# One TensorE loop of eight rounds and new column shares for the DMA engines in a grouped 1x1 convolution

## The chip, the cores and the metric

The kernel runs on one core of one Trainium2 chip. The metric is the device time of one execution in microseconds (us). Most runs of one kernel agree within some 0.3%. Every experiment was timed in turns with the kernel before on the same chip. A ratio is always the mean time of one kernel's fast runs over that of the other's of the same rounds, so it is not quite the ratio of the medians quoted beside it.

## The reference

```python
H = W = 512; G = 4; Cg = 48; C = 192; k = 1
# x: (1, 512, 512, 192) bf16,  w: (1, 1, 4, 48, 48) bf16
xg = x.reshape(B, H, W, G, Cg)
out = einsum('bhwgc,gcd->bhwgd', xg, w[0, 0]).reshape(B, H, W, C)
```

Each of the 262,144 pixels has four groups of 48 channels, and each group is multiplied by its own 48x48 matrix. 100.7 MB are read and as many written, with little arithmetic for each byte.

## The kernel before

Pixels are spread over 128 SBUF rows (partitions). A "column" is one pixel on every row, 384 bytes in each. Loads go into a ring of three slots of 80 columns. Four columns are a "group" of the program: 6 transposes and 6 matmuls on TensorE, and one copy by ScalarE into an output ring of 280 columns, from which stores leave. Two groups are a "pair", the unit of TensorE's program; VectorE makes one copy for each pair, between the transposes and the matmuls.

Three parts matter here. First, the column plan. Most pieces have all 128 rows. The PARTIAL pieces leave out rows 16 to 19 and 48 to 51, so that these eight rows get fewer pixels; a REST piece gives 12 columns more to rows 0 to 15 alone:

```python
FULL = (("sync", 0, 128, 128),)
PARTIAL = (                                   # queue, first row, rows, outer
    ("sync", 0, 16, 4), ("sync", 32, 16, 4),
    ("pool", 52, 44, 11), ("pool", 20, 12, 3), ("pool", 96, 32, 8),
)
REST = (("sync", 0, 16, 4),)
FRONT = ((6, ((36, FULL), (44, PARTIAL))), (12, ((12, REST), (24, FULL), (44, PARTIAL))))
```

Second, the TensorE program. In this program a loop is possible only where every slot is one regular load of 80 columns, because the loop's wait for a slot has to be the same in each round. The mixed slots (36 + 44, and 12 + 24 + 44) break this, so there are two loops, of 2 and of 4 rounds of 30 pairs; 138 of the 258 pairs' instructions are written out:

```python
                for pair in range(pair, first):
                    step(pair)
                with pe.Fori(0, rounds):
                    for pair in range(first, first + body):
                        step(pair)
```

Third, the waits. TensorE waits for each piece's own semaphores at the piece's first group:

```python
                    if g == p.g0:
                        keys = [ld_key[p.i, n] for n in range(len(p.blocks))]
                        for key in keys:
                            pe.wait_ge(ld_sem[key], 16)
                        todo += keys if p.regular else []
```

## Time and profile before

The kernel before takes 479.06 us (median of 3 runs, 478.95 to 479.91). The profiled span is 477.7 us.

| what | value | read from |
|---|---|---|
| packets' time, all DMA queues | 99% of 16 engines' span | page, part 3 |
| TensorE busy, ScalarE busy | 430.9 us, 390.1 us | page, part 1 |
| fetches of TensorE instructions | 26 of 16 KB | page, part 3, queue q8 |
| ScalarE waits for stores to leave the output ring | 21.7 us | view of waits |
| TensorE waits for loads | 7.3 us (matmuls); the weight loads' 4.0 us is the longest of these waits seen once more | view of waits |

The page of the kernel before. PE and ACT are TensorE and ScalarE, PEld is TensorE's loading of weights, DVE is VectorE and POOL is GpSimd; the rows of part 2 are 40 equal slices of the span in tenths; part 3 has for each queue its packets, MB and share of the 16 engines' time.

```profile
span 477.7 us, 13632 instructions
PE 430.9 (90%) x6202; PEld 389.3 (81%) x6202; DVE 247.8 (52%) x259; ACT 390.1 (82%) x517; POOL 12.5 (3%) x28
DMA  8999999999999999999999999999999999999997
q1 hardware_dynamic: 4340, 97.71, 48.0%
q10 hardware_dynamic: 4996, 97.69, 47.9%
q0 software_dynamic: 1216, 5.95, 3.0%
q8 instruction: 26, 0.43, 0.3%
```

The DMA row has no hole: loads (q1), stores (q10) and the transfers of the partial pieces (q0) fill the 16 engines from start to end. Queue q8, of the kind "instruction", is taken for the one that brings TensorE's instructions: its packets have 16,384 bytes each. One such transfer is called a fetch here.

The view of waits of the kernel before, in us in total, times, and longest:

```profile
PEld o_ps L339 <- ACT oring L415: 60.1, 149, 3.7
ACT oring L415 <- DMA out_dram<-oring: 21.7, 10, 3.5
PE xT_ps L319 <- DMA ring<-in_x_dram: 7.3, 4, 3.8
PEld xT_ps L319 <- DMA ring<-in_x_dram: 4.0, 1, 4.0
```

The two kinds of wait on DMA are what compute's slack is spent on.

### The profile page before, as it was taken

Reading aid. Unit: us, or ns where it says so; the run is one execution under the profiler, and the core shown is the slowest. Engines: PE = TensorE matmul, PEld = TensorE weight load, DVE = VectorE, ACT = ScalarE, POOL = GpSimd, SP = SyncE. Lnnn points to the kernel's source line nnn. Section 1 sums busy time; section 2 is a strip of 40 time slices with the busy share of each in tenths; the row PEclk is TensorE's granted clock in tenths of the full one; section 3 lists DMA queues with packets and bytes.
Section 4 is the critical chain, followed back from the end, with each engine's and each line's share of the span. In section 5 each row is a group of like instructions: output and inputs, shape, how many; then the busy total and the mean of one; then the engine's idle time right before and its main releaser. Section 6 shows DMA issues by size and latency. Waiting matters only on the chain.

```text
span 477.7 us, 13632 instructions
## 1 busy us (share of the span) xinstructions
PE 430.9 (90%) x6202; PEld 389.3 (81%) x6202; DVE 247.8 (52%) x259; ACT 390.1 (82%) x517; POOL 12.5 (3%) x28
## 2 busy tenths in 40 slices
PE   5999999999986999999897997899997969979994
PEld 4988889888876898888796896789886868878883
DVE  2555555555543555555553554455554534635551
ACT  2898899988984998998895886799987858868885
POOL 1000000200002000000000000002000020000000
PEclk9999999999998999999998999999999989989997
DMA  8999999999999999999999999999999999999997
GB/s 325 445 403 432 417 426 429 438 427 431 427 428 432 437 420 433 425 436 430 434 434 423 435 435 433 430 429 430 425 431 430 428 426 433 420 432 429 423 401 302
DMA packets 10588, 201.85 MB, mean 423 GB/s; under 512 B 2105, under 2 KB 2105, under 8 KB 2649
## 3 DMA queue, kind: packets, MB, share of 16 engines
q1 hardware_dynamic: 4340, 97.71, 48.0%
q10 hardware_dynamic: 4996, 97.69, 47.9%
q0 software_dynamic: 1216, 5.95, 3.0%
q8 instruction: 26, 0.43, 0.3%
q14 instruction: 10, 0.07, 0.0%
HBM read 100.68 MB, written 100.66 MB: 421 GB/s over the span
## 4 chain that ended last, share of the span: by engine, by line
PE 56%; DMA 30%; ACT 9%; another core or an unknown queue 2%; issue 1%; ACTq 1%; SPq 0%
PE o_ps L339 32%; PE xT_ps L319 23%; DMA out_dram<-oring 21%; DMA ring<-in_x_dram 9%; ACT oring L415 9%; ACTq L396 1%; SPq L288 0%; SPq L281 0%; ACTq L389 0%; ACTq L398 0%
## 5 line engine op out<-in xcount | busy, mean ns | idle before, releaser
L415 ACT CAST oring<-o_ps 128x768 bf16<-128x768 f32 x516 | 388.8, 801 | 81.6 <-PE o_ps L339 53.0
L378 DVE COPY xT_sb<-xT_ps 128x1536 bf16<-128x1536 bf16 x258 | 247.1, 958 | 218.7 <-PE xT_ps L319 218.7
L339 PE MATMUL o_ps<-wt,xT_sb 128*128 128x144 bf16 (+1 forms) x3096 | 289.7, 236 | 30.4 <-ACT oring L415 25.0
L339 PEld LDWEIGHTS o_ps<-wt,xT_sb 128*128 128x128 bf16 x3096 | 212.7, 99 | 69.0 <-ACT oring L415 60.1
L319 PE MATMUL xT_ps<-ident,ring 128*128 128x128 bf16 x3096 | 222.3, 222 | 7.3 <-DMA ring<-in_x_dram 7.3
L319 PEld LDWEIGHTS xT_ps<-ident,ring 128*128 128x128 bf16 x3096 | 190.0, 99 | 10.2 <-DMA ring<-in_x_dram 4.0
L260 POOL DMA_DIRECT2D fill<-in_x_dram x8 | 4.6, 574 | 376.2 <-PE xT_ps L319 258.6
L268 POOL DMA_DIRECT2D ring<-in_x_dram x6 | 3.3, 560 | 0.0
L275 POOL DMA_DIRECT2D out_dram<-oring x6 | 3.3, 556 | 0.0
L300 PE MATMUL o_ps<-w_sb,esel 48*128 48x48 bf16 x10 | 0.6, 209 | 2.6 <-DMA w_sb<-in_w_dram 2.6
L300 PEld LDWEIGHTS o_ps<-w_sb,esel 48*128 48x128 bf16 x10 | 0.4, 111 | 2.6 <-POOL esel L247 2.6
L371 DVE CAST wt<-o_ps 128x480 bf16<-128x480 f32 x1 | 0.7, 657 | 3.2 <-PE o_ps L300 3.2
L415 ACT ACT_TABLE_LOAD x1 | 1.3, 1283 | 0.8 <-PEq L435 0.8
L247 POOL TENSOR_SCALAR_AFFINE_SELECT esel<-esel 48x272 bf16<-48x272 bf16 x1 | 0.4, 402 | 0.0
L244 POOL MEMSET esel<- 48x272 bf16 x1 | 0.3, 317 | 0.3 <-POOLq L435 0.3
L251 POOL TENSOR_SCALAR_AFFINE_SELECT ident<-ident 128x128 bf16<-128x128 bf16 x1 | 0.3, 282 | 0.0
L245 POOL MEMSET ident<- 128x128 bf16 x1 | 0.2, 197 | 0.0
L435 POOL MEMSET const-float32-0.0<- 128x1 f32 x1 | 0.1, 98 | 0.3 <-issue 0.3
L435 POOL MEMSET const-bfloat16-1.0<- 128x1 bf16 x1 | 0.1, 101 | 0.0
L435 POOL MEMSET const-uint8-127<- 128x1 uint8 x1 | 0.1, 101 | 0.0
L435 POOL MEMSET const-float32-1.0<- 128x1 f32 x1 | 0.1, 98 | 0.0
## 6 DMA issues: line engine op xcount, KB each, us to landing
ring<-in_x_dram SPq DMA_DIRECT2D x22, 3840.0 KB, 28.8
out_dram<-oring ACTq DMA_DIRECT2D x12, 3456.0 KB, 39.9
out_dram<-oring ACTq DMA_DIRECT2D x11, 3264.0 KB, 44.7
out_dram<-oring ACTq DMA_DIRECT2D x2, 2880.0 KB, 48.3
out_dram<-oring ACTq DMA_DIRECT2D x2, 1728.0 KB, 31.3
ring<-in_x_dram SPq DMA_DIRECT2D x1, 3072.0 KB, 21.6
ring<-in_x_dram SPq DMA_DIRECT2D x2, 1152.0 KB, 17.0
ring<-in_x_dram SPq DMA_DIRECT2D x1, 2304.0 KB, 11.1
```

What stands on the lines that cost most here:

```text
L247: gp.affine_select(out=esel[:], in_=esel[:], pattern=[[-1, ECOLS]], compare_op=AluOpType.is_equal, fill=0.0, base=ESHIFT, channel_multipli ...
L260: gp.dma_start(dst, src).then_inc(fill_sem[k], 16)
L268: gp.dma_start(sbuf, dram).then_inc(ld_sem[ld_key[p.i, n]], 16)
L275: gp.dma_start(dram, sbuf).then_inc(st_sem[i][n], 16)
L300: last = pe.matmul(o_ps[:, NOB - 1, col:col + CG], lhsT=esel[:, s0:s0 + 128], rhs=w_sb[:, g, :], start=True, stop=True, skip_group_check=True)
L319: last = pe.transpose(xT_ps[:, g % NXP, j * 128:(j + 1) * 128], xg[:, j * 128:(j + 1) * 128], ident[:])
L339: last = pe.matmul(o_ps[:, v % NOB, c0_:c1_], lhsT=xs[:, j * 128:(j + 1) * 128], rhs=wt[:, WOFF[tc]:WOFF[tc] + (c1_ - c0_)], start=(tc == ...
L371: dve.tensor_copy(wt[:], o_ps[:, NOB - 1, 0:WCOLS]).then_inc(wc_sem, 1)
L378: dve.tensor_copy(xT_sb[pair % NXS][:, 0:n * 2 * UC].rearrange("p (g c) -> p g c", g=n), xT_ps[:, b0:b0 + n, 0:2 * UC]).then_inc(e_done[pa ...
L396: act.dma_start(dram, sbuf).then_inc(st_sem[i][n], 16)
L415: act.copy(out_columns(g).rearrange("p (u c) -> p u c", u=2), o_ps[:, v % NOB:v % NOB + 2, 0:UC]).then_inc(fa_done[g % (2 * NTOK)] if g < ...
L435: nc = _bacc.Bacc("TRN2", target_bir_lowering=False, num_devices=1)
```

## The change

The intent: make the mixed slots look regular to TensorE, so that one loop of 8 rounds covers nearly the whole program. GpSimd waits for all DMAs of a mixed slot and then counts the slot's ordinary semaphore up. The partial pieces get 48 columns instead of 44. They now come first in their slot. The second has 16 columns fewer on rows 0 to 15, which also makes the pixel count come out. The rule that cuts the stores changes too; with the new columns the late ones come out finer. The core of the diff:

```diff
 PARTIAL = (
-    ("sync", 0, 16, 4), ("sync", 32, 16, 4),
-    ("pool", 52, 44, 11), ("pool", 20, 12, 3), ("pool", 96, 32, 8),
+    ("sync", 0, 16, 4, 0), ("sync", 32, 16, 4, 0),
+    ("pool", 52, 44, 11, 0), ("pool", 20, 12, 3, 0), ("pool", 96, 32, 8, 0),
 )
-REST = (("sync", 0, 16, 4),)
-FRONT = ((6, ((36, FULL), (44, PARTIAL))), (12, ((12, REST), (24, FULL), (44, PARTIAL))))
+UNEVEN = (("sync", 0, 16, 4, 16), *PARTIAL[1:])
+FRONT = ((6, ((48, PARTIAL), (32, FULL))), (11, ((48, UNEVEN), (32, FULL))))
 ... (a Unit is a slot with all its pieces; loop_spans now goes by units)
+                for p in u.pieces:                      # GpSimd
+                    for n in range(len(p.blocks)):
+                        gp.wait_ge(ld_sem[ld_key[p.i, n]], 16)
+                gp.sem_inc(ld_sem[unit_keys[u][0]], 16)
 ...
-                    if g == p.g0:                       # TensorE
-                        keys = [ld_key[p.i, n] for n in range(len(p.blocks))]
-                        for key in keys:
+                    if g == u.g0:
+                        for key in unit_keys[u]:
                             pe.wait_ge(ld_sem[key], 16)
-                        todo += keys if p.regular else []
+                        todo += unit_keys[u] if u.regular else []
 ... (stores: OGRID ends at least 24 columns on; short full fields in one store)
```

There are now 514 groups in 257 pairs, of which 47 are written out.

More of the change, by code (lines that the diff above doesn't have):

```diff
@@ L37 @@
 NTOK = 6
-FULL = (("sync", 0, 128, 128),)
+FULL = (("sync", 0, 128, 128, 0),)
 PARTIAL = (
-    ("sync", 0, 16, 4), ("sync", 32, 16, 4),
-    ("pool", 52, 44, 11), ("pool", 20, 12, 3), ("pool", 96, 32, 8),
-)
-REST = (("sync", 0, 16, 4),)
-FRONT = ((6, ((36, FULL), (44, PARTIAL))), (12, ((12, REST), (24, FULL), (44, PARTIAL))))
+    ("sync", 0, 16, 4, 0), ("sync", 32, 16, 4, 0),
+    ("pool", 52, 44, 11, 0), ("pool", 20, 12, 3, 0), ("pool", 96, 32, 8, 0),
+)
+UNEVEN = (("sync", 0, 16, 4, 16), *PARTIAL[1:])
+FRONT = ((6, ((48, PARTIAL), (32, FULL))), (11, ((48, UNEVEN), (32, FULL))))
 FILL_ROWS = 5
@@ L58, in __init__ @@
         self.blocks = []
-        for (queue, r0, rows, outer) in blocks:
-            self.blocks.append((queue, r0, rows, outer, pix))
-            pix += rows * cols
+        for (queue, r0, rows, outer, less) in blocks:
+            self.blocks.append((queue, r0, rows, outer, pix, cols - less))
+            pix += rows * (cols - less)
         self.pix_end = pix
@@ L73, in __init__ @@
         self.full, self.blocks = field.full, field.blocks
-        self.regular = self.full and size == BIG and self.at % BIG == 0
         assert size % 4 == 0 and self.at + size <= RCOLS
@@ L90, in plan_fields @@
         head = 0
-    cols = npix - sum(n * sum(b[2] for b in blocks) for n, blocks in parts)
+    cols = npix - sum((n - b[4]) * b[2] for n, blocks in parts for b in blocks)
     if cols < 128 * BIG:
@@ L128, in plan_stores @@
             if f.full:
-                end = min([g for g in OGRID if g > at]) - at + c
+                end = min([g for g in OGRID if g > at + 24] or [OCOLS]) - at + c
+                if f.cols < BIG:
+                    end = min(OCOLS - at + c, f.cols)
                 if ends and c >= f.cols - LATE_COLS:
@@ L137, in plan_stores, with __init__, plan_units, loop_spans @@
     return stores
-def loop_spans(pieces):
+class Unit:
+    def __init__(self, pieces):
+        self.pieces, self.g0, self.g1 = pieces, pieces[0].g0, pieces[-1].g1
+        self.slot = pieces[0].at // BIG
+        self.regular = pieces[0].at % BIG == 0 and 4 * (self.g1 - self.g0) == BIG
+def plan_units(pieces):
+    units, rest = [], list(pieces)
+    while rest:
+        n = 1
+        if rest[0].g0 and rest[0].at % BIG == 0:
+            while n < len(rest) and rest[n].at % BIG:
+                n += 1
+        units.append(Unit(rest[:n]))
+        rest = rest[n:]
+    return units
+def loop_spans(units):
     body, out, run = RCOLS // 4, [], []
-    for p in pieces + [None]:
-        if p and p.regular:
-            run.append(p)
+    for u in units + [None]:
+        if u and u.regular:
+            run.append(u)
             continue
@@ L165, in bass_standalone__grouped__vision_kernel @@
     stores = plan_stores(fields)
-    piece_of = {g: p for p in pieces for g in range(p.g0, p.g1)}
+    units = plan_units(pieces)
+    unit_of = {g: u for u in units for g in range(u.g0, u.g1)}
     store_of = {g: s for s in stores for g in range(s.g0, s.g1)}
@@ L169, in bass_standalone__grouped__vision_kernel @@
     NP = (NG + 1) // 2
-    LOOPS = loop_spans(pieces)
+    LOOPS = loop_spans(units)
     assert all(RCOLS // 4 % n == 0 for n in (2 * NXS, 2 * NTOK, NXP))
@@ L181, in transfers @@
         f, c0, c1, at = part.field, part.c0, part.c1, part.at
-        for n, (queue, r0, rows, outer, pix) in enumerate(f.blocks):
+        for n, (queue, r0, rows, outer, pix, cols) in enumerate(f.blocks):
             if queue not in queues:
                 continue
-            px = ap[pix:pix + rows * f.cols, :]
+            px = ap[pix:pix + rows * cols, :]
             if f.full:
@@ L190, in transfers @@
                 view = px.rearrange("(c a i) n -> a c (i n)", a=outer, c=rows // outer)
-            yield n, view, tile[r0:r0 + rows, at * C:(at + c1 - c0) * C]
-    ld_key = {}
-    for p in pieces:
-        for n in range(len(p.blocks)):
-            ld_key[p.i, n] = (p.at // BIG,) if p.regular else ("piece", p.i, n)
-    partial = [p for p in pieces if any(b[0] == "pool" for b in p.blocks)]
+            yield n, view, tile[r0:r0 + rows, at * C:(at + (c1 - c0 if f.full else cols)) * C]
+    ld_key, unit_keys = {}, {}
+    for u in units:
+        whole = u.regular and len(u.pieces) == 1 and u.pieces[0].full
+        for p in u.pieces:
+            for n in range(len(p.blocks)):
+                ld_key[p.i, n] = ("slot", u.slot) if whole else ("piece", p.i, n)
+        unit_keys[u] = [("slot", u.slot)] if u.regular else [ld_key[p.i, n] for p in u.pieces for n in range(len(p.blocks))]
+    mixed = [u for u in units if u.regular and unit_keys[u] != [ld_key[u.pieces[0].i, 0]]]
     with ExitStack() as es:
@@ L208, in bass_standalone__grouped__vision_kernel @@
         wt = es.enter_context(nc.sbuf_tensor("wt", [128, WCOLS], BF16))
-        fill = es.enter_context(nc.sbuf_tensor("fill", [FILL_ROWS, 32 * max(1, len(partial))], BF16))
+        fill = es.enter_context(nc.sbuf_tensor("fill", [FILL_ROWS, 32 * max(1, len(mixed))], BF16))
         xT_ps = es.enter_context(nc.psum_tensor("xT_ps", [128, NXP, 1024], BF16))
@@ L214, in sem @@
             return es.enter_context(nc.semaphore(name))
-        ld_sem = {k: sem("ld_" + "_".join(map(str, k))) for k in sorted(set(ld_key.values()), key=str)}
+        ld_sem = {k: sem("ld_" + "_".join(map(str, k))) for k in sorted({*ld_key.values(), *sum(unit_keys.values(), [])}, key=str)}
         st_sem = [[sem(f"st{i}_{n}") for n in range(len(s.field.blocks))] for i, s in enumerate(stores)]
@@ L225, in bass_standalone__grouped__vision_kernel @@
         go_sem = sem("go_sem")
-        fill_sem = [sem(f"fill{k}") for k in range(4 * len(partial))]
+        fill_sem = [sem(f"fill{k}") for k in range(4 * len(mixed))]
         def columns(g):
-            p = piece_of[g]
-            at = p.at + 4 * (g - p.g0)
+            at = 4 * g % RCOLS
             return ring[:, at * C:(at + 4) * C]
@@ L261, in filler @@
                 used.append(k)
-            for nth, p in enumerate(partial):
-                gp.wait_ge(t_done, freed(p))
-                for n, dram, sbuf in transfers(xf, ring, p, ("pool",)):
-                    if n in FILL_BEFORE:
-                        filler()
-                    gp.dma_start(sbuf, dram).then_inc(ld_sem[ld_key[p.i, n]], 16)
+            for nth, u in enumerate(mixed):
+                part = [p for p in u.pieces if not p.full]
+                for p in part:
+                    gp.wait_ge(t_done, freed(p))
+                    for n, dram, sbuf in transfers(xf, ring, p, ("pool",)):
+                        if n in FILL_BEFORE:
+                            filler()
+                        gp.dma_start(sbuf, dram).then_inc(ld_sem[ld_key[p.i, n]], 16)
+                for p in u.pieces:
+                    for n in range(len(p.blocks)):
+                        gp.wait_ge(ld_sem[ld_key[p.i, n]], 16)
+                gp.sem_inc(ld_sem[unit_keys[u][0]], 16)
                 gp.wait_ge(go_sem, nth + 1)
                 for i, s in enumerate(stores):
-                    if s.field is p.field:
+                    if any(s.field is p.field for p in part):
                         for n, dram, sbuf in transfers(of, oring, s, ("pool",)):
@@ L306, in transposes @@
                 for g in groups(pair):
-                    p = piece_of[g]
+                    u = unit_of[g]
                     if g % 2 and pair:
                         pe.wait_ge(e_done[(pair - 1) % NTOK], 1)
-                    if g == p.g0:
-                        keys = [ld_key[p.i, n] for n in range(len(p.blocks))]
-                        for key in keys:
+                    if g == u.g0:
+                        for key in unit_keys[u]:
                             pe.wait_ge(ld_sem[key], 16)
-                        todo += keys if p.regular else []
+                        todo += unit_keys[u] if u.regular else []
                     xg = columns(g)
```

## The prediction

> **What bounds the kernel now.** DMA throughput. The page gives two hardware queues 48.0% and 47.9% and the software queue 3.0% of 16 engines' span: 99.2% with instruction fetches. Its slices stand at 9 except the first and last, at about 430 GB/s. PE is busy 430.9 of 477.7 us, ACT 390.1. Between waits ACT does 20 groups in 16.5 us (timeline), so 516 groups need about 426 us plus some 15 us of start and tail: compute has about 35 us of slack, spent in waits for loads (PE, 11 us) and for stores leaving the output ring (ACT, 21.7 us in the view of waits).
>
> In the trace's DMA packets a 30,720-byte packet takes 1,138 ns on nearly all engines (27 GB/s). One unbroken chain of packets is slower by 45 to 60 ns in each, some 20 us in all. It carries no software-queue data while the partial pieces move, so I take it for the engine of the skipped rows 16 to 19 and 48 to 51. [...] Today it is spared 88 columns x 8 rows x 384 B, both ways: 0.54 MB, 20 us. The last store's 16 landings lie within 1.8 us: the balance is good.
>
> **What the change does.**
> - Bytes: unchanged, 201.3 MB. The spared engine is spared 96 columns instead of 88. The four engines of rows 0 to 15 lose 12 extra columns and get 16 fewer: estimate -2.3 us each. The other eleven get 2056 instead of 2052 columns: +0.9 us each; the spared one -0.9 us.
> - Program: pairs written out fall from 138 to 47 (loops of 2 and 4 rounds of 30 pairs become one of 8). The trace has 26 fetches of 16 KB, 0.94 us each, spread over engines, none during repeated rounds. I expect 8 to 11: about 15 us less over 16 engines, estimate -1 us each.
> - Compute: 514 groups instead of 516, -1.65 us, mostly in slack.
> - Waits: PE now waits for a whole slot (48 partial + 32 full columns) through GpSimd, no longer starting on 36 full columns first. I expect a PE stall of 1 to 7 us near 130 us in place of the 5 us at 145 us. GpSimd's counting up costs under 1 us, twice. Both hide: queued loads and stores keep DMA at 1.0.
> - Tail: the last 56 groups run at compute's pace from 425 us; four engines end 0.3 to 1.8 us late. If these serve rows 0 to 15, they are relieved.
>
> **On the critical path.** Fewer fetches -1, the eleven engines +0.9, tail relief 0 to -2: net about -1 us, -0.3%.
>
> **Prediction.** 478.0 us, from 474.0 to 482.0 (8 in 10). Faster by over 2%: 0.03; within 2%: 0.94; slower by over 2%: 0.03.
>
> **What would show it.** Queue shares again sum to 99%; instruction packets on the fetch queue fall to about 10; one PE wait on a semaphore from GpSimd near 130 us, none near 145; DMA slices stay at 9; ACT's total wait for stores stays near 20 us; last landing spread at most 2 us.
>
> **What would make it wrong.** The slot-wide wait starving both queues (DMA slices under 0.9); repeated rounds fetching instructions again; the spared engine having become too idle or the eleven others too loaded, so that the last landing spread exceeds 3 us.

The sum: -1, +0.9 and 0 to -2 us came to about -1 us, from 479.06 to 478.0 us.

## The result

The changed kernel takes 477.94 us (median of 4 runs, 477.73 to 478.14) against 479.13 us before (a fourth run is in this median). The ratio is 0.9972, with a 95% interval of 0.9955 to 0.9989. Run again on another chip it took 478.11 us, ratio 0.9978 (0.9959 to 0.9997). So there is a small real gain of about a quarter of a per cent, 1.2 us. What was expected of the second run:

> The changed kernel itself, as the yardstick on this chip. Expected 0.9972 of before: 477.7 to 478.3 us. Packet by packet its 9 fetches fall only on 8 of the 16 DMA engines (one of them twice), and that engine should land last again.

The page and the view of waits of the changed kernel, the lines that answer to those above:

```profile
span 476.1 us, 13580 instructions
PE 431.7 (91%) x6178; PEld 389.5 (82%) x6178; DVE 246.8 (52%) x258; ACT 388.3 (82%) x515; POOL 12.5 (3%) x28
DMA  8999999999999999999999999999999999999996
q1 hardware_dynamic: 4320, 97.44, 48.0%
q10 hardware_dynamic: 5120, 97.42, 47.8%
q0 software_dynamic: 1216, 6.49, 3.3%
q8 instruction: 9, 0.15, 0.1%
```

```profile
PEld o_ps L370 <- ACT oring L446: 54.3, 152, 3.8
ACT oring L446 <- DMA out_dram<-oring: 15.2, 7, 3.4
PEld xT_ps L350 <- POOLq L300: 5.1, 1, 5.1
PE xT_ps L350 <- POOLq L300: 4.9, 1, 4.9
PE xT_ps L350 <- DMA ring<-in_x_dram: 2.9, 2, 1.5
```

The DMA row is as full as before. Fetches fell from 26 to 9. The new wait on GpSimd (POOLq) is there, once, 5.1 us long (both lines of it are the same wait, seen by weight loads and by matmuls). It replaces the longest wait for a load. The second mixed slot had landed in time and makes no wait at all.

### Which engine each packet ran on

The page averages over 16 DMA engines. To see one engine, the packet records were chained: the next packet on an engine was taken to start 3 or 4 ns before the last one ends (by far the commonest distances: in the kernel before, 5,858 pairs of a start and an end lie 4 ns apart in this way, 5,328 lie 3 ns and 363 lie 1 ns), and each queue's packet sizes to come in the order of its DMAs. This follows 16 chains through nearly the whole trace. Two chains that end in the same nanosecond can be exchanged, so single chains are less sure than groups of them. The chains fall into four groups:

- four that carry the two small SyncE parts of the partial pieces: rows 0 to 15 and 32 to 47;
- one that carries no part of a partial piece: the spared rows 16 to 19 and 48 to 51. Its packets are longer than the others' of the same size, by 17 us in sum, and most of that is in the stores: in the changed kernel the median store packet of 27,648 bytes takes 1,098 ns there and 1,025 on the others, the median load packet of 30,720 bytes 1,154 and 1,138;
- eleven with the software queue's data, and of these, *eight that got every single instruction fetch of TensorE, in turn, while three got none*.

That the spared rows are one engine's is read from the sizes in the chains: one chain lacks exactly what the partial pieces leave out. The packet times, which need no chain, agree. In the kernel before, 8 of the 128 store packets of 15,360 bytes, one engine's share, are 6 to 12% longer than the median of 573 ns; of the 480 packets of 16,896 bytes in the partial pieces (median 629 ns) only four are over 2% longer. The SyncE parts there, four sets of 32 such packets, never have more than four in flight at once.

Packet time of one engine, mean of each group, from 6 us after the start (us), and when the last packet ended. Own reading of the packet records of the profiled runs:

```
                 fetches   four   eight   three   spared   last end, in group
before              26     470.8  471.4   467.6   464.0    476.8 eight (4 fetches)
changed              9     467.8  469.5   468.2   464.8    475.2 eight (2 fetches)
changed, again       9     468.6  469.8   468.3   463.6    475.3 eight (2 fetches)
two loops           25     468.2  472.0   468.2   463.6    477.7 eight (4 fetches)
no loop             48     469.0  476.1   469.1   464.1    480.5 eight
no loop, direct     48     469.1  476.6   468.4   464.9    481.2 eight
```

A fetch holds its engine for 0.94 us in the mean (26 packets of the kernel before), so 17 fetches fewer over eight engines are 2.0 us on each of the eight, and nothing on the others. The change gives the eight 4 columns more (0.9 us: 24,576 bytes both ways, at the 1,138 ns of a 30,720-byte packet) and the four much less. The measured differences of the groups, changed less before, are -1.9 for the eight, -3.0 for the four, +0.6 for the three and +0.8 for the spared one.

The 16 landings of the last store (us from the span's start), from the semaphore records:

```
before   475.4 475.4 475.4 475.4 475.4 475.4 475.4 475.4 475.5 475.5 475.5 475.5 475.7 476.2 476.8 477.2
changed  470.6 470.6 470.9 472.0 472.3 472.4 473.0 473.1 473.1 473.3 473.7 473.8 474.0 474.0 474.2 475.6
```

Before, twelve engines waited idle for the last store, which ScalarE could issue only at 472.5 us, and two engines, those with four fetches, ended last. Afterwards ScalarE ends at 467.7 us, nobody waits for it, and the engine with two fetches ends last. In the changed kernel run again ScalarE ended later, at 469.9 us, five engines waited for the last store (they ended at 472.5 to 472.6), and the engine with two fetches ended last again. So compute's end moves by 2 us between these two runs, while the engine that lands last is the same kind.

### The profile page after: what moved, and what is told of

It is laid out like the page before. It is cut to its first block, busy times and chain, and to the rows that moved or that the text cites. A ratio compares the mean times of both kernels' runs of the same rounds, so it can differ in the third digit from the quotient of the medians.

```text
span 476.1 us, 13580 instructions
## 1 busy us (share of the span) xinstructions
PE 431.7 (91%) x6178; PEld 389.5 (82%) x6178; DVE 246.8 (52%) x258; ACT 388.3 (82%) x515; POOL 12.5 (3%) x28
## 4 chain that ended last, share of the span: by engine, by line
PE 48%; DMA 39%; ACT 8%; ACTq 1%; issue 1%; another core or an unknown queue 1%; SPq 0%; POOLq 0%
DMA out_dram<-oring 29%; PE o_ps L370 28%; PE xT_ps L350 20%; DMA ring<-in_x_dram 9%; ACT oring L446 8%; ACTq L427 1%; SPq L320 0%; SPq L313 0%; ACTq L420 0%; POOLq L300 0%; POOLq L299 0%; ACTq L429 0%
## 5 line engine op out<-in xcount | busy, mean ns | idle before, releaser
L350 PEld LDWEIGHTS xT_ps<-ident,ring 128*128 128x128 bf16 x3084 | 190.1, 100 | 10.9 <-POOLq L300 5.1
```

Source lines behind the costliest of these rows:

```text
L350: last = pe.transpose(xT_ps[:, g % NXP, j * 128:(j + 1) * 128], xg[:, j * 128:(j + 1) * 128], ident[:])
```

## The experiments

Theory A: the gain comes from the instruction fetches, which take time from the DMA engines, and more than their mean over 16 engines says, as only eight engines are hit and the slowest engine ends the kernel. The new column shares are needed beside it, because without them other engines become the last. Theory B: the columns and late stores make the gain, and fetches are hidden. Rival C, about a cost: the slot-wide wait and the counting up on GpSimd cost time, which another part of the change pays for. The new rule for the stores was never tested alone: no run has the new columns without it.

The first two runs were expected from the mean over 16 engines, before the chains had been followed.

### The two old loops with the new columns

```diff
-    LOOPS = loop_spans(units)
+    LOOPS = [(9, 30, 2), (79, 30, 4)]
```

> The new column plan, waits and stores, but the TensorE program written out as before: loops of 2 and 4 rounds instead of one of 8. Theory A (the gain is mostly the fetches that fell from 26 to 9, each holding one of 16 DMA engines for 0.95 us): 25 to 27 fetches again, packet time over all engines up by 15 to 25 us, time up by 0.8 to 1.6 us against the changed kernel, so 478.7 to 479.5 us. Theory B (the gain comes from the new column shares and late stores): 26 fetches but within 0.3 us of the changed kernel's 477.9.

Measured: 480.26 us, ratio to before 1.0018 (1.0005 to 1.0031). Against the changed kernel's 0.9978 on another chip that is 0.4% or 1.9 us more, from 16 fetches more. Theory B falls. The size is twice what a mean over 16 engines gives (14.9 us of packet time / 16 = 0.9), and what a mean over eight gives (1.9).

```profile
q8 instruction: 25, 0.41, 0.3%
```

The table above shows the eight at 472.0 against 468.2 for their neighbours.

### No loop at all

```diff
-    LOOPS = loop_spans(units)
+    LOOPS = []
```

> The changed kernel without any loop: all 257 pairs written out, some 50 fetches of 16 KB. Theory A: 41 fetches more than the changed kernel, 39 us of packet time more over 16 engines, so 2.4 us on the mean and up to 3.5 us on the last engine: 480.3 to 481.5 us. Theory B: no more than 0.5 us over the changed kernel.

Measured: 483.26 us, ratio 1.0086 (1.0073 to 1.0100), so 1.1% or 5.2 us over the changed kernel. That is outside what was expected of theory A with 16 engines.

```profile
q8 instruction: 48, 0.79, 0.6%
PEld xT_ps L350 <- issue: 3.5, 2, 1.9
```

39 fetches more are 37.8 us of packet time: 2.4 us over 16 engines, 4.7 us over eight. The eight ended between 479.3 and 480.5 us, the eight others at 477.6 to 477.7, idle until the last store came. The kernel with two loops ran on the same chip in the same rounds: 23 fetches (22.9 us of packet time) and 3.0 us lie between these two, where eight engines give 2.9 us and sixteen 1.4.

A rival would be that TensorE itself stalls at a fetch. The second line above counts its waits for which the profile shows no releaser ("issue"): 3.5 us in two waits with 48 fetches, both in the first 20 us. In the changed kernel, with 9, it reads:

```profile
PEld xT_ps L350 <- issue: 3.2, 2, 1.6
```

TensorE's own waits did not grow with the fetches, so the time is lost in the DMA engines. Whatever the branches back in the loop cost, it is less than the fetches that they save: without them the kernel is 5.2 us slower.

### The old columns with the one loop

```diff
-UNEVEN = (("sync", 0, 16, 4, 16), *PARTIAL[1:])
-FRONT = ((6, ((48, PARTIAL), (32, FULL))), (11, ((48, UNEVEN), (32, FULL))))
+REST = (("sync", 0, 16, 4, 0),)
+FRONT = ((6, ((36, FULL), (44, PARTIAL))), (12, ((12, REST), (24, FULL), (44, PARTIAL))))
... (and the stores' rule of before)
```

> The columns and the stores of the kernel before (36 full + 44 partial; 12 extra + 24 + 44), but the new slot-wide counting up and the one loop of 8 rounds. Theory A: 9 fetches, 1 us less than before: 477.9 to 478.3. Theory B: within 0.3 us of before (479.1), as the columns are unchanged. If the loop alone gives more than the whole change (under 477.6), the new columns cost.

Measured: 479.48 us, ratio 1.0003 (0.9985 to 1.0022): no gain, although the fetches are down to 9. Theory A in its simple form missed here by about 1.2 us. The chains tell why: the four engines of rows 0 to 15 need 471.2 us of packet time with the 12 extra columns, the others some 468, and the two last ends are two of the four, 476.0 and 476.9 us; the next is 473.8. These two carry small instruction fetches besides (8 KB, queue q14; 309 ns each in the median, before and changed). Taking fetches from the eight gives nothing when engines of the four are as late as the eight were. By the medians the loop and the columns pay only together: the columns with the new stores and waits cost 0.2% (two loops), the loop with the old columns gives 0.0%, both give -0.25%. The times alone do not prove the second of these, as the interval of this run overlaps those of the changed kernel; the chains carry it.

### The relief moved to other rows

The pixel count needs 256 pixels fewer in the second partial piece. They are taken from rows 96 to 127 (8 columns) instead of rows 0 to 15 (16 columns), once with one loop and once with two.

```diff
-UNEVEN = (("sync", 0, 16, 4, 16), *PARTIAL[1:])
+UNEVEN = (*PARTIAL[:-1], ("pool", 96, 32, 8, 8))
```

> The changed kernel, but the 256 missing pixels are taken as 8 columns from rows 96 to 127 (eight engines) instead of 16 columns from rows 0 to 15 (four engines). In the changed kernel 3 or 4 engines end about 2 us before the mean, so I think they are the relieved ones. If the last engine sets the end: the four get 1.8 us more, eight others 0.9 us less, the last landings lie closer (5.0 us spread becomes 3 to 4), and the time falls by 0 to 0.9 us, 477.0 to 477.9. If compute set the end: unchanged at 477.9.

> The changed kernel with the two old loops (26 fetches) and the relief on rows 96 to 127 instead of rows 0 to 15. With one loop that move cost time (478.9 against about 478.1). Theory A2 (fetches hit only eight engines, the ones of rows 64 to 127, and the slowest engine ends the kernel): here the eight are the last by 2 us, so relieving them by 8 columns on 4 rows (0.9 us) must help: 479.2 to 479.8 against 480.3 with the relief on rows 0 to 15. Theory B (rows 0 to 15 are the ones that need relief in any case): slower again, 481 or more.

Measured: with one loop 478.88 us, ratio 0.9982 (0.9969 to 0.9994), no faster than the changed kernel; with two loops 479.36 us, ratio 1.0007 (0.9987 to 1.0027), against 1.0018 with the relief on rows 0 to 15. The first expectation, a gain of up to 0.9 us, was a miss. The signs are those of theory A (the move helps where the eight are late, and doesn't where the four are), but both differences lie inside the intervals, so the times alone don't settle it. The chains do more: with one loop the last ends are those of two engines of the four, 476.4 and 476.9 us, which also carry the small instruction fetches. That run's ScalarE also ended late, at 472.7 us against 467.7, so not all of its time is the four engines' doing.

The second expectation took the eight engines with fetches for those of rows 64 to 127. The chains speak against it. The shorter piece of rows 96 to 127 marks its engines, as its packets have 15,360 bytes instead of 18,432. In the run with two loops the fetches go round the same eight chains in the same order from 17 to 460 us, and only six of these eight carry marked packets. The other two fetch chains carry none, and two marked chains get no fetch. The run of the middle way below, with marks of 16,896 bytes, gives six and two as well. So this relief reached six of the eight engines that needed it, which may be why it helped little.

A middle way, 8 columns fewer on rows 0 to 15 and 4 on rows 96 to 127:

```diff
-UNEVEN = (("sync", 0, 16, 4, 16), *PARTIAL[1:])
+UNEVEN = (("sync", 0, 16, 4, 8), *PARTIAL[1:-1], ("pool", 96, 32, 8, 4))
```

> Between the changed kernel and the moved relief: 8 columns fewer on rows 0 to 15 and 4 fewer on rows 96 to 127. In the changed kernel the engine with two fetches ends last by about 0.5 to 1.3 us before the engines of rows 0 to 15 that carry small instruction fetches. Estimate: fetch engines 0.46 us earlier, the four engines 0.9 us later. If the balance sets the end, 477.7 to 478.7, between the 478.1 and the 478.9 of the two ends; a gain over the changed kernel of more than 0.5 us would surprise me.

Measured: 477.73 us, ratio 0.9960 (0.9944 to 0.9977). It is the lowest ratio, but the interval overlaps those of the changed kernel (0.9972 and 0.9978), and on this chip six runs spread from 477.17 to 479.08. It is certainly faster than the kernel before; that it beats the changed kernel is not shown. Its ratio is 0.6 to 0.9 us better, which is more than the 0.5 us that was to be a surprise.

### No partial pieces

```diff
-FRONT = ((6, ((48, PARTIAL), (32, FULL))), (11, ((48, UNEVEN), (32, FULL))))
+FRONT = ()
```

> The changed kernel with no partial pieces: 128 full rows everywhere, no GpSimd transfers, one loop, 512 groups. If one engine is slow by itself (17 us of extra packet time in the changed kernel) it now gets back 0.59 MB, 22 us at 26.8 GB/s, and ends alone and last: 490 to 496 us. If its slowness comes from the software queue, it goes away with it, all engines are even, and the kernel takes 475 to 478 us.

Measured: 490.15 us, ratio 1.0222 (1.0203 to 1.0241). One engine needs 483.5 us of packet time, 18.0 us of it because its packets are longer, where the other 15 need 466 to 471; it lands the last store at 488.0 us, five us after all others. No GpSimd DMA runs in this kernel (its page has no q0), so the software queue is not what makes this engine slow. What does is open. Sparing it is worth 12 us, ten times the change studied here. The page also shows the DMA row thinning out in the last three slices. ScalarE waited 34.3 us for stores in this run (15.2 in the changed kernel) and issued the last store at 479.5 us, so the 15 other engines ran out of queued work early:

```profile
DMA  8999999999999999999999999999999999999754
q8 instruction: 8, 0.13, 0.1%
```

### Waiting for pieces directly

The kernel without a loop again, but TensorE waits for each piece of a mixed slot itself, and GpSimd neither waits nor counts up.

```diff
-                    if g == u.g0:
+                    if u in mixed:
+                        for p in u.pieces:
+                            for n in range(len(p.blocks) if g == p.g0 else 0):
+                                pe.wait_ge(ld_sem[ld_key[p.i, n]], 16)
+                    elif g == u.g0:
... (GpSimd's waits and its sem_inc taken out)
```

> The kernel without any loop, but TensorE waits for each piece of a mixed slot itself, at that piece's first group; GpSimd does not wait and does not count up. Theory A (the slot-wide wait and the counting up hide in compute's slack): within 0.6 us of the 483.3 of the kernel without a loop. Rival C (they cost): 482.3 or less.

Measured: 484.00 us, ratio 1.0098 (1.0081 to 1.0114), against 1.0086 with the counting up. Direct waits gain nothing: rival C falls for the kernel without a loop. (The run is 0.7 us above that kernel's 483.26 on another chip, just outside the 0.6 us that were expected; the two intervals overlap.)

### The counting up made late

Twelve dummy memsets on GpSimd between a mixed slot's landing and its counting up. (A first form with larger memsets did not build: its tile had no room in SBUF: it needed 4,096 B and 1,664 B were left.)

```diff
+                for k in range(LATE_N):
+                    gp.memset(late[:], 0.0).then_inc(late_sem, 1)
+                    gp.wait_ge(late_sem, LATE_N * nth + k + 1)
                 gp.sem_inc(ld_sem[unit_keys[u][0]], 16)
```

> The changed kernel with twelve dummy memsets of 128x512 on GpSimd, one after the other, between the landing of a mixed slot and GpSimd's counting up, so that TensorE starts both mixed slots several us later (estimate 0.5 us each, 6 us; the trace will say). Theory A (the wait hides, as queued loads and stores keep the 16 DMA engines busy): within 0.6 us of the changed kernel's 478.1, with two TensorE waits on GpSimd of about 11 us each. Rival C (the wait is paid in full): 12 us more, 490; half paid: 484.

Measured: 478.56 us, ratio 0.9974 (0.9954 to 0.9994), the same as the changed kernel. The memsets took 525 ns each, 6.3 us a slot. The view of waits and the DMA row of this run:

```profile
PEld xT_ps L356 <- POOLq L306: 14.9, 2, 10.9
ACT oring L452 <- DMA out_dram<-oring: 7.8, 2, 5.9
DMA  8999999999999999999999999999999999999997
```

TensorE waits 14.9 us for GpSimd instead of 5.1 (10.9 and 4.0 us, where two waits of 11 were expected), ScalarE waits 7.8 us for stores instead of 15.2, and the DMA row is as full as ever. A wait moved from one place to another, and the DMA engines, which bound the kernel, stayed as busy.

### The weights put together by DMA

In the changed kernel the ninth fetch comes at 467 us, when TensorE is at its end, and falls on the engine that had the first. This run drops 20 TensorE instructions by building the weights with ten small DMAs on the ScalarE queue.

```diff
-            build_weights()
+            act.wait_ge(p0_sem, 1)
+            for (tc, r, g, c0_) in WBLOCKS:
+                lo, hi = max(r, 0), min(r + CG, 128)
+                col = WOFF[tc] + c0_
+                act.dma_start(wt[lo:hi, col:col + CG], wv[lo - r:hi - r, g, :]).then_inc(wc_sem, 16)
```

> The changed kernel, but the block-diagonal weights are put together by ten small DMAs into a zeroed tile, instead of ten matmuls and a copy: 20 TensorE instructions fewer. In the changed kernel the ninth fetch comes at 467 us, when TensorE has all but ended, and falls on the engine that had the first one, which then lands last. If 20 instructions are enough to keep the program under that boundary: 8 fetches, one for each of the eight engines, last landing 0.5 to 1.3 us earlier, 476.8 to 477.6. If not: 9 fetches and 477.6 to 478.6.

Measured: 496.63 us, ratio 1.0364 (1.0350 to 1.0378), a plain failure, and the fetches stayed at 9. The view of waits and the page's rates in the 40 slices show where the 18 us went:

```profile
PEld xT_ps L334 <- DMA wt<-in_w_dram: 25.5, 1, 25.5
DMA  9931999999999999999999999999999999999997
GB/s 359 436 162 42 384 433 428 426 427 427 430 436 425 435 432 428 425 438 432 434 427 434 433 430 431 433 427 426 439 429 430 430 415 429 435 427 440 420 417 308
```

The ten DMAs move 36 KB in all (sum of the issue lines), but the last landed at 31.1 us. In the changed kernel's packet records from 200 to 300 us, 1,189 of the 1,193 successions of loads and stores that can be told apart (the next packet 2 to 5 ns before the end of one, with no rival) go from a load packet to a store packet or back: there the engines took turns between the two queues packet by packet. If they did so here, each 96-byte packet had to wait for a load packet of 30,720 bytes (1.14 us) on the same engine. That is the estimate, as this run's packets were not followed one by one; the spacing of the landings, 1.4 to 4.6 us for each DMA of 16 to 48 rows (one to three an engine if they spread evenly), fits it. In the changed kernel the weights are the first transfer on the load queue and land at 2.6 us. The three slots filled, then the DMA engines stood still for about 18 us (from 30 to 48 us) because TensorE had freed no slot. This is what a wait looks like that does not hide: a hole in the DMA row.

## Why the prediction was right or wrong

The time was predicted at 478.0 us and came out at 477.94. That is partly luck: the sum was right with two wrong terms in it. The fetches were put too low (-1 instead of -2.0 us), and a relief of the tail by 0 to 2 us, which did not come in this form, made up for it.

- **DMA bounds the kernel: right.** Packet shares sum to 99% before and after. Changes in waits left the time alone (late counting up, direct waits); changes of packet time on the slowest engines moved it (no loop, no partial pieces).
- **Fetches fall from 26 to 8 to 11: right** (9), and no fetch comes in repeated rounds: between 71 and 458 us the changed kernel has none, while a loop of 30 pairs, 1,440 weight loads and matmuls, runs its 8 rounds.
- **"estimate -1 us each": this step failed.** It spread 15 us over 16 engines. The chains show every fetch on eight engines, so the term was -2.0 us on the eight, two of which ended last, and nothing on the others. No loop, with 5.2 us for 39 fetches, shows the size in time: eight engines give 4.7, sixteen 2.4; against two loops in the same rounds it is 3.0 us, where eight give 2.9 and sixteen 1.4.
- **"The other eleven get 2056 instead of 2052 columns: +0.9 us each": right as far as it goes.** The three without fetches went up by 0.6 us. Together with the fetches the eight went down by 1.9 us in the profiled runs, where 2.0 - 0.9 = 1.1 us were due; the rest are long single packets that differ from run to run (the changed kernel run again: 1.6).
- **"The four engines of rows 0 to 15 ... -2.3 us each": the right direction**; 3.0 and 2.2 us less in the two runs of the changed kernel. **"The spared one -0.9": not seen**, +0.8 and -0.4; such a term is within what one engine varies from run to run.
- **"Slower by 45 to 60 ns in each": too even.** On that chain the median load packet is 14 ns longer and the median store packet of 27,648 bytes 73 ns (kernel before); the engine is slow mainly where it stores.
- **"four engines end 0.3 to 1.8 us late. If these serve rows 0 to 15": wrong.** By the chains, the two last had four fetches each, the third was one of the four, the next one of the eight. The relief of rows 0 to 15 is needed all the same, but for another reason: with the eight relieved by the loop, two of the four would have become the last (old columns with one loop: no gain).
- **The wait: right.** One wait of 5.1 us near 130 us, none near 145, hidden. Even 14.9 us of it stayed hidden. GpSimd's counting up, put at under 1 us, took 43 ns each time (at 129.0 and 338.5 us).
- **"ACT's total wait for stores stays near 20 us": missed**, 15.2. **"last landing spread at most 2 us": missed**, 5.0 us, and 2.9 in the run again, where the last store came later and hid part of it. By the prediction's own sign, over 3 us, the shares are now less even: the spared engine and two of the four end 5 us before the last. The kernel gained all the same, as the last of the eight ends earlier: the last landing is at 475.6 us instead of 477.2.

What stays open: why fetches fall on eight engines only, and which rows two of these eight serve (six are engines of rows 96 to 127, by the marked packets); what makes one engine's packets longer; what the new rule for the stores is worth alone; and whether the middle share of relief beats the changed kernel.

## What to carry to other kernels

With all DMA engines full, the slowest one set the time here (with no partial pieces one engine landed 5 us after the rest and cost 12 us), so cost a change on each engine and not as a share of 16: instruction fetches that are 0.3% of the packet time moved this kernel by twice their mean (1.9 us for 16 of them, where the mean gives 0.9), as they fell on half of the engines. A smaller TensorE program was then worth something although TensorE had slack (busy 431.7 of 476.1 us; 39 fetches cost 5.2 us). Taking load off one group of engines paid only where the next group was not just as late, which is how the chains explain that the loop gave nothing with the old columns. A wait on a compute engine was free here while the DMA row of the page stayed at 9 (14.9 us of it), and it was paid for where it opened a hole (18 us).
